# A banded attention, router and expert kernel: the exponential one group later, routing steps behind the maxima and in front of weights' low halves

## The chip, the cores and the metric

The kernel runs on one core of a Trainium2 chip. The metric is the device time of one execution in microseconds (us); lower is better. The engines are named as in the profile: PE is TensorE (matrix products; PEld its weight loads), DVE is VectorE, ACT is ScalarE, POOL is GpSimd, SP is the engine that only issues DMAs. Each engine takes its instructions in the order in which the program gave them.

## The reference, cut to what matters

Three stages in a row, with batch 4, sequence 576 and width 512:

```python
# 8 heads of 64; a band of 32 keys, heads 4 to 7 with a dilation of 4
scores = where(mask, q @ k.T / 8, -1e9)
attn = exp(scores - max) / (sum + 1e-9)
x = (attn @ v)                                  # (4, 576, 512)

# 8 experts of 512 x 1024 x 512, one per token
logits = x @ w_gate                             # gate from x @ w_local
e = argmax(logits[b, s]) if s == 0 or sigmoid(x @ w_local) < 0.5 else prev_e
x = p[e] * (relu(x @ w1[e]) @ w2[e])            # p = softmax(logits)

# a causal convolution of 5 taps as a gate
out = (sigmoid(conv(x)) * (x @ w_val)) @ w_out
```

The expert of a token can be that of the token before it, so the router holds a running maximum over the sequence; then the tokens of each expert are counted and gathered.

## The kernel before

**Attention.** The work is 8 iterations `it` (a pair of batches and a pair of heads each), each cut into five groups, so 40 groups (`NG`); a group has two slices of 128 queries, the fifth one. The loop at L1036 runs over `t`, the group whose scores are made, and in each turn works on several groups at different stages:

- `stage_a(t)` (L558): the score products into PSUM tile `s`, then on DVE one masked maximum per head and slice (L576, written `CUSTOM_DVE_ANT_0` with its `DVE_READ_ACCUMULATOR2_ANT` in the profile, `ISA` in the order), four in a group of two slices. They write `sm` and `mx`.
- `transpose_qk` for the next iteration: transposes of q and k on PE; k's are copied into `kbd` by ACT (L550, L553).
- `stage_sub(t)` (L580): POOL subtracts the maxima (L584). POOL also copies the q tiles of later iterations (`qside`, L489) and issues the gathers of tokens (L325).
- `stage_d` and `stage_l` (L641, L652): the finished attention rows are transposed, copied to `xT` by ACT (L650), and multiplied with the router's weights into `lp` (L661).
- `stage_b(t - 2)` (L594): transposes of the exponentials `pb` into `pt`, copied to `ph` by ACT or DVE (L603, L605).
- `stage_c(t - 3)` (L621): the product with v into `o`; after three slices `o_evac` (L609) normalises with three DVE instructions (`rc`, `rc`, `xsb`).
- `shift_v` (L511), a copy on ACT, in two groups of five; then `stage_exp(t)` (L587), the exponential on ACT, which needs POOL's subtraction of the same group.

So ACT's order in a turn is `kbd`, `xT`, `ph` of group t - 2, the shift, the exponential of group t, then high halves of weights.

**Routing among it.** `route(0)` (L762) is the router's work for the first two batches, begun at group `START` = 25. It gives small DVE instructions to a list (`Later`, L685). `later.tick(n)` takes the next n off the list and issues them: one after each maximum (L577), one after each step of the normalisation (L614, L616, L619), and `REST` = 3 at the end of a turn (L1147). In a profile they carry L716 or L701. Between them stand four products on PE (`lg`, `wp`, `bt`, `tb`); how many of the three calls of `later.passed()` in a turn must pass before a product's result is copied out of PSUM is `EVACUATE` = 2. The last of these products, `tb`, gives the table `tab`, from it the indices `idxa` by which tokens are gathered, and `eka2`, the number of the second expert.

**The first expert's weights.** Each expert has eight pieces of 128 x 1024 in f32, loaded into three slots `wst` (SP, L262, L265) and split in two f16 halves: ACT makes the high half `wh` (`split_a`, L274), DVE the low half `wl` (`split_b`, L279), which frees the slot, so that the load three pieces on is issued. `SPLIT` gives for each piece the groups at whose end the two are issued, the low halves (`finish_splits`) in front of the `REST` routing steps. The tokens come by POOL's gathers at groups 36, 37, 37 and 39, are transposed (`xt`, L337) and split (`xh`, `xl`); the first expert product `h` (L356) is issued at group 42.

After the attention come the experts, L356 and L405, and the last stage (L1427 to L1542). Nothing of their order is touched.

Of the kernel before, what the change touches and what calls it, by code (L numbers as in the profile page):

```python
# [53 lines left out]
BUSY = 40  # L54
RELIEF = 6
FILL = (6, 16)
SPLIT = ((34, 35), (34, 35), (35, 36), (37, 38), (38, 39), (39, 42), (41, 43), (41, 42), (45, 46), (47, 48), (48, 50), (51, 52), (52, 57), (55, 59), (57, 61), (61, 63))
GATHERS = (36, 37, 37, 39)
TURNS = (39, 40, 40, 43)
UP = (42, 43, 44, 44, 45, 46, 46, 47)  # L60
# [4 lines left out]
PREP = (18, 20, 22)  # L65
PLACES = (1, 2, 0, 0)
LAGS = (0, 3, 0, 2, 0, 0, 2)
EVACUATE = 2
START = 25
REST = 3  # L70
TICKS = (8, 6, 7, 4)
# [91 lines left out]
def attention_moe_conv_kernel(ctx: ExitStack, tc: tile.TileContext, q, k, v, w_gate, w_local, w1, w2, w_val, conv_w, w_out, consts, out):  # L163
# [112 lines left out]
    def split_b(k, i):  # L276
        wh, wl = wt[k, i]
        st = wf.pop((k, i))
        V.scalar_tensor_tensor(out=wl, in0=st, scalar=SW, in1=wh, op0=ALU.mult, op1=ALU.subtract)  # L279

    def start_splits(t):
        for n, (at, _) in enumerate(SPLIT):
            if t == at:
                split_a(2 * (n // 8), n % 8)

    def finish_splits(t):
        for n, (_, at) in enumerate(SPLIT):
            if t == at:
                split_b(2 * (n // 8), n % 8)
                k, i = 2 * ((n + 3) // 8), (n + 3) % 8  # L290
                if n + 3 < 16:
                    fetch_w(k, i, evs[k])
# [145 lines left out]
    if True:  # L438
# [15 lines left out]
        for n in range(2):  # L454
            flat = lv.tile([P, W + 4 * S], F32, name=f"kbd{n}")
            (V if n == 0 else G).memset(flat[:, 0:W], 0.0)
            t = flat[:, W:].rearrange("c (b h s) -> c b h s", b=2, h=2)
# [6 lines left out]
        def pair(it):  # L464
            return it // 4, PR[it // 4][it % 4]
# [89 lines left out]
        def scores(nm):  # L555
            return sp.tile([P, 2, 2, KB], F32, tag="s", name=nm)

        def stage_a(g):  # L558
            it, sl = groups[g]
            bp, pr = pair(it)  # L560
            dil = pr >= 2
            qT, (kb, front) = qk[it]
            qf = qT.rearrange("c b s -> c (b s)")
            ps = scores(f"s{g}")
            for n, s in enumerate(sl):
                for half in range(2):
                    blk = 2 * s + half
                    bl, i = divmod(blk, NB)
                    T.matmul(ps[64 * half : 64 * half + 64, n, :, :], lhsT=qf[:, QB * blk : QB * blk + QB], rhs=kb[:, bl, :, ks[i] : ks[i] + KB] if i else front[:, bl, :, 0:KB], start=True, stop=True)  # L569
            sm = wk.tile([P, 2, 2, KB], F32, tag="sm", name=f"sm{g}")  # L570
            mx = wk.tile([P, 4], F32, tag="mx", name=f"mx{g}")
            for n, s in enumerate(sl):
                mi = 3 + s if dil else (0 if s == 0 else 2 if s == 4 else 1)
                for h in range(2):
                    u = 2 * n + h
                    V.tensor_tensor_reduce(out=sm[:, n, h, :], in0=ps[:, n, h, :], in1=masks[:, KB * mi : KB * mi + KB], scale=0.125, scalar=-3e38, op0=ALU.add, op1=ALU.max, accum_out=mx[:, u : u + 1])  # L576
                    later.tick()  # L577
            stiles[g] = sm, mx

        def stage_sub(g):  # L580
# [6 lines left out]
        def stage_exp(g):  # L587
            ns = len(groups[g][1])
            smf = ptiles[g]
            pb = wk.tile([P, 4, KB], F32, tag="pb", name=f"pb{g}")  # L590
            A.activation(out=pb[:, 0 : 2 * ns, :], in_=smf, func=AF.Exp)
            ptiles[g] = pb
# [16 lines left out]
        def o_evac(it, part):  # L609
            bp, pr = pair(it)  # L610
            o = otile.pop((it, part))
            r = wk.tile([P, 3, 2], F32, tag="rc", name=f"rc{it}{part}")
            V.tensor_scalar(out=r, in0=o[:, :, :, HD], scalar1=1e-9, scalar2=None, op0=ALU.add)
            later.tick()  # L614
            V.reciprocal(out=r, in_=r)
            later.tick()  # L616
            xo = xsb[bp, pr >= 2][:, 3 * part : 3 * part + 3, P * (pr % 2) : P * (pr % 2) + P].rearrange("p s (h d) -> p s h d", h=2)
            V.tensor_tensor(out=xo, in0=o[:, :, :, 0:HD], in1=r.unsqueeze(3).to_broadcast([P, 3, 2, HD]), op=ALU.mult)
            later.tick()  # L619

        def stage_c(g):  # L621
            it, sl = groups[g]
# [62 lines left out]
        class Later:  # L685
# [55 lines left out]

            def passed(self):
                self.passes += 1
                if self.passes >= EVACUATE:
                    self.early()

            def slot(self):
# [11 lines left out]
        later = Later()  # L759
# [233 lines left out]
        NG = len(groups)  # L993
# [16 lines left out]
        with tc.manual_schedule():  # L1010
# [25 lines left out]
            for t in range(NG + 5):  # L1036
# [22 lines left out]
                    later.start(route(0))  # L1059
                later.passed()  # L1060
                later.product(0)
                if 0 <= t - 2 < NG:
                    stage_b(t - 2)

# [11 lines left out]
                if t < NG:  # L1076
                    if gi in ((1, 4) if it < 5 else (0, 3)):
                        shift_v(it, gi // 3)
                    stage_exp(t)
                start_splits(t)  # L1080

                if gi == 0 and 0 < it and it + 1 < 8:
# [54 lines left out]
                for j in (0, 2):  # L1137
                    if f"expert{j}" in later.marks and (j == 0 or t >= EXPERT2):
                        later.marks.remove(f"expert{j}")
                        evs[j] = nc.values_load(eka[j][0:1, 0:1], engines=[ET.SP], min_val=0, max_val=E - 1)  # L1140
                        for i in range(0 if j else 3):
                            fetch_w(0, i, evs[0])
                finish_splits(t)
                if "places" in later.marks:
                    later.marks.remove("places")
                    assert t <= GATHERS[0]
                later.tick(REST)  # L1147
                events(t)
                for at in UP:
                    if t == at and t < 44:  # L1150
# [482 lines left out]
```

## Time and profile before

| | before |
|---|---|
| median of 3 runs | 455.64 us (455.29 to 455.97) |
| the profiled execution | 456.03 us |
| its span, first to last instruction | 454.2 us |
| PE busy | 435.0 us, 96% of the span |
| DVE busy | 337.5 us, 74% |
| ACT busy | 291.9 us, 64% |
| POOL busy | 161.6 us, 36% |

All times inside the kernel are from the span's start. The attention and the first router take up to about 129 us, the experts up to about 340, the last stage the rest. Busy shares are means over these stages; what an engine waits for is read within a stage.

### The profile page before, as it was taken

The page shows a single profiled execution, that of the slowest core. Times are in us where ns is not written, and L with a number is a line of the kernel's source. Part 1 is how long each engine was busy: PE and PEld are TensorE (multiplying, and loading weights), DVE is VectorE, ACT ScalarE, POOL GpSimd, SP SyncE. Part 2 cuts the span into 40 slices and gives each one's busy share as a digit, 9 for nine tenths or more (in the row PEclk, how much of TensorE's full clock was granted, in tenths as well). Part 3 has the DMA queues.
Part 4 walks back from the last instruction along what each step waited for, and adds up shares of the span by engine and source line. Part 5 has one row for each costly group of instructions (what it writes and reads, how often), then busy time and mean ns, then how long its engine had stood idle before and what let it go on. Part 6 is the DMA issues. An engine that isn't in the chain of part 4 may idle for free. (4 is left out here: it accounts for less than half of the span.)

```text
span 454.2 us, 12091 instructions
## 1 busy us (share of the span) xinstructions
PE 435.0 (96%) x4618; PEld 324.1 (71%) x4618; DVE 337.5 (74%) x981; ACT 291.9 (64%) x590; POOL 161.6 (36%) x190
## 2 busy tenths in 40 slices
PE   8889999988699999999999999999999999999997
PEld 7567777766476688876788888788685757566664
DVE  5767787996788845788979999997038888779730
ACT  3877888766755434556566766766357998786532
POOL 3666655421600244102215133242115745434130
PEclk9999999996899999999999999999999999999999
DMA  9976698564847494366878898981052423020202
GB/s 207 202 178 150 156 244 200 143 182 137 253 116 277 174 319 150 114 239 221 218 271 286 280 316 240 312 262 36 9 175 84 150 70 105 25 93 5 91 23 94
DMA packets 56870, 77.32 MB, mean 170 GB/s; under 512 B 25810, under 2 KB 34146, under 8 KB 56808
## 3 DMA queue, kind: packets, MB, share of 16 engines
q1 hardware_dynamic: 53432, 66.72, 49.9%
q0 software_dynamic: 3232, 9.72, 6.2%
q8 instruction: 38, 0.62, 0.6%
q14 instruction: 24, 0.20, 0.1%
q10 hardware_dynamic: 144, 0.07, 0.1%
HBM read 62.19 MB, written 14.30 MB: 168 GB/s over the span
## 5 line engine op out<-in xcount | busy, mean ns | idle before, releaser
L356 PE MATMUL h<-xh,wh 128*128 128x256 f16 (+9 forms) x352 | 86.4, 256 | 1.4 <-DVE hl L360 1.2
L356 PE MATMUL h<-xl,wh 128*128 128x256 f16 (+9 forms) x352 | 86.4, 255 | 0.1
L356 PE MATMUL h<-xh,wl 128*128 128x256 f16 (+9 forms) x352 | 86.4, 256 | 0.0
L279 DVE SCALAR_TENSOR_TENSOR wl<-wst,wh 128x1024 f16<-128x1024 f32 x64 | 77.9, 1220 | 10.7 <-ACT wh L274 10.6
L1480 DVE SCALAR_TENSOR_TENSOR acc<-y,cw,acc 128x288 f32<-128x288 f32 x128 | 65.6, 520 | 9.2 <-ACT acc L1454 6.3
L356 PEld LDWEIGHTS <-wh 128*128 128x128 f16 x704 | 64.2, 98 | 9.4 <-issue 2.9
L274 ACT ACTIVATE wh<-wst 128x1024 f16<-128x1024 f32 x64 | 66.9, 1050 | 1.6 <-DMA wst<-in_moe_w_dram 1.6
L358 ACT ACTIVATE hh<-h 128x256 f16<-128x256 f32 (+9 forms) x88 | 30.6, 348 | 40.7 <-PE h L356 38.1
L360 DVE SCALAR_TENSOR_TENSOR hl<-h,hh 128x256 f16<-128x256 f32 (+9 forms) x88 | 32.4, 376 | 25.8 <-ACT hh L358 25.2
L584 POOL TENSOR_TENSOR sm<-sm,mx 128x384 f32<-128x384 f32 (+1 forms) x40 | 31.6, 792 | 51.6 <-DVE mx L576 32.5
L367 POOL DMA_INDIRECT yD<-yr,idx x15 | 18.1, 1208 | 82.6 <-ACT yr L366 54.9
L405 PE MATMUL yf<-wh,hh 128*128 128x512 f16 x104 | 39.4, 379 | 0.1
L405 PE MATMUL yf<-wh,hl 128*128 128x512 f16 x104 | 39.4, 379 | 0.0
L405 PE MATMUL yf<-wl,hh 128*128 128x512 f16 x104 | 39.4, 379 | 0.0
L1510 PE MATMUL v<-yh,wv_h 128*128 128x288 f16 x128 | 36.6, 286 | 0.3 <-DVE gg L1519 0.2
L1510 PE MATMUL v<-yh,wv_l 128*128 128x288 f16 x128 | 36.6, 286 | 0.0
L1510 PE MATMUL v<-yl,wv_h 128*128 128x288 f16 x128 | 36.6, 286 | 0.0
L356 PEld LDWEIGHTS <-wl 128*128 128x128 f16 x352 | 34.4, 98 | 2.5 <-issue 0.2
L405 PEld LDWEIGHTS <-hh 128*128 128x128 f16 x208 | 20.3, 98 | 21.1 <-issue 0.6
L576 DVE CUSTOM_DVE_ANT_0 sm<-s,masks 128x96 f32<-128x96 f32 x144 | 29.7, 251 | 6.8 <-PE s L569 5.5
L569 PE MATMUL s<-kbd,qT 128*64 128x192 f32 x288 | 31.8, 333 | 2.8 <-ACT kbd L553 2.0
L389 PEld LDWEIGHTS <-wh 128*128 128x128 f16 x576 | 32.9, 97 | 2.2
(248 smaller groups left out, 1052.7 us busy)
## 6 DMA issues: line engine op xcount, KB each, us to landing
wst<-in_moe_w_dram SPq DMA_DIRECT2D x64, 512.0 KB
qraw<-in_q_dram SPq DMA_DIRECT2D x16, 288.0 KB
kraw<-in_k_dram SPq DMA_DIRECT2D x16, 288.0 KB
out_dram<-ob SPq DMA_DIRECT2D x17, 256.0 KB
yg<-yD SPq DMA_DIRECT2D x16, 256.0 KB
xD<-xsb SPq DMA_DIRECT2D x2, 1152.0 KB
lraw<-in_moe_w_val_dram SPq DMA_DIRECT2D x4, 512.0 KB
lraw<-in_moe_w_out_dram SPq DMA_DIRECT2D x4, 512.0 KB
```

Of the source, the lines that this page charges most:

```text
L274: A.activation(out=wh, in_=st, func=AF.Copy, scale=SW)
L279: V.scalar_tensor_tensor(out=wl, in0=st, scalar=SW, in1=wh, op0=ALU.mult, op1=ALU.subtract)
L356: T.matmul(ps[:, :n], lhsT=w[:, fs], rhs=x[:, cc, :], start=q == 0, stop=q == 11)
L358: A.activation(out=hh[:, fc, :], in_=ps[:, :n], func=AF.Relu)
L360: V.scalar_tensor_tensor(out=hl[:, fc, :], in0=ps[:, :n], scalar=0.0, in1=hh[:, fc, :], op0=ALU.max, op1=ALU.subtract)
L389: T.matmul(ps[:, :r], lhsT=w[:, ds_], rhs=x[:, fc, r0:n], start=q == 0, stop=q == 23)
L405: T.matmul(ps, lhsT=x[:, fc, t0 : t0 + P], rhs=w[:, (fc % 2) * D : (fc % 2) * D + D], start=q == 0, stop=q == 23)
L569: T.matmul(ps[64 * half : 64 * half + 64, n, :, :], lhsT=qf[:, QB * blk : QB * blk + QB], rhs=kb[:, bl, :, ks[i] : ks[i] + KB] if i else f ...
L576: V.tensor_tensor_reduce(out=sm[:, n, h, :], in0=ps[:, n, h, :], in1=masks[:, KB * mi : KB * mi + KB], scale=0.125, scalar=-3e38, op0=ALU. ...
L584: G.tensor_tensor(out=smf, in0=smf, in1=mx[:, 0 : 2 * ns].unsqueeze(2).to_broadcast([P, 2 * ns, KB]), op=ALU.subtract)
L1480: V.scalar_tensor_tensor(out=acc, in0=y32[:, cc, s0 + k : s0 + k + hw], scalar=cw[:, cc, k : k + 1], in1=acc, op0=ALU.mult, op1=ALU.add)
L1510: T.matmul(ps, lhsT=w[:, cc, cs], rhs=x[:, cc, hs], start=q == 0, stop=q == 11)
```

## The change

1. `stage_exp(t)` at the end of a turn becomes `stage_exp(t - 1)` in the next turn, in front of `stage_b(t - 2)`.
2. The ticks after the single maxima are taken together after a group's last maximum, and those between the steps of the normalisation after its last step. The number of ticks is the same.
3. The `REST` routing steps stand in front of the low halves of the turn, not behind them.
4. In `SPLIT`, the low halves of pieces 1 and 2 of the first expert move from groups 35 and 36 to 36 and 37.
5. `EVACUATE` becomes a table by product: 2, 2, 2 and for the fourth 1.

```diff
-SPLIT = ((34, 35), (34, 35), (35, 36), (37, 38), (38, 39), (39, 42), ...
+SPLIT = ((34, 35), (34, 36), (35, 37), (37, 38), (38, 39), (39, 42), ...
-EVACUATE = 2
+EVACUATE = (2, 2, 2, 1)
...
                     V.tensor_tensor_reduce(out=sm[:, n, h, :], ...
-                    later.tick()
+            later.tick(2 * len(sl))
...
             V.tensor_scalar(out=r, in0=o[:, :, :, HD], scalar1=1e-9, scalar2=None, op0=ALU.add)
-            later.tick()
             V.reciprocal(out=r, in_=r)
-            later.tick()
...
             V.tensor_tensor(out=xo, in0=o[:, :, :, 0:HD], ...
-            later.tick()
+            later.tick(3)
...
-                if self.passes >= EVACUATE:
+                if self.passes >= EVACUATE[min(self.made, 4) - 1]:
...
                 later.product(0)
+                if 0 < t <= NG:
+                    stage_exp(t - 1)
                 if 0 <= t - 2 < NG:
                     stage_b(t - 2)
...
                         shift_v(it, gi // 3)
-                    stage_exp(t)
                 start_splits(t)
...
-                finish_splits(t)
+                later.tick(REST)
                 if "places" in later.marks:
                     later.marks.remove("places")
                     assert t <= GATHERS[0]
-                later.tick(REST)
+                finish_splits(t)
                 events(t)
```

ACT around group 34, before: the shift of v, then the exponential of group 33 (`pb33` from `sm33`), then what the turn of group 34 needs.

```order
L514 COPY vraw3False_1888<-vraw3False_1888 32x2x8x64
L591 ACTIVATE pb33_2073<-sm33_2033 128x384
L553 COPY kbd1_149<-tpk7_7_2087 64x288 x2
L650 COPY xT5_1931<-tpx52_2094 128x384
L603 COPY ph32_2104<-pt32_2099 96x512
L591 ACTIVATE pb34_2119<-sm34_2083 128x192
L274 ACTIVATE wh0_0_2121<-wst0_0_2017 128x1024
L274 ACTIVATE wh0_1_2124<-wst0_1_2019 128x1024
```

The same place in the changed kernel:

```order
L514 COPY vraw3False_1886<-vraw3False_1886 32x2x8x64
L553 COPY kbd1_149<-tpk7_7_2085 64x288 x2
L648 COPY xT5_1929<-tpx52_2092 128x384
L591 ACTIVATE pb33_2097<-sm33_2031 128x384
L603 COPY ph32_2104<-pt32_2099 96x512
L274 ACTIVATE wh0_0_2119<-wst0_0_2015 128x1024
L274 ACTIVATE wh0_1_2122<-wst0_1_2017 128x1024
L591 ACTIVATE pb34_2168<-sm34_2081 128x192
L603 COPY ph33_2175<-pt33_2170 96x512
```

The two copies into `kbd` and the copy into `xT` now stand ahead of the exponential of group 33, and two high halves ahead of that of group 34.

DVE at the end of group 35 and the start of group 36, before: the normalisation, the copy of the table, two low halves, then the place list and the first maximum.

```order
L613 TENSOR_SCALAR rc61_2185<-o6_1_2114 128x6
L615 RECIPROCAL rc61_2185<-rc61_2185 128x6
L618 TENSOR_TENSOR xsb6_2062<-o6_1_2114,rc61_2185 128x3x128
L716 COPY tab_78<-tb0_2153 128x48
L279 SCALAR_TENSOR_TENSOR wl0_0_2122<-wst0_0_2017,wh0_0_2121 128x1024
L279 SCALAR_TENSOR_TENSOR wl0_1_2125<-wst0_1_2019,wh0_1_2124 128x1024
L716 TENSOR_TENSOR pra_2190<-sel_112,tab_78 128x32
L701 TENSOR_REDUCE idxa_2191<-pra_2190 128x4
L576 ISA sm36_2225,mx36_2226<-s36_2220,masks_64 128x96
L576 ISA mx36_2226 128x1
L716 TENSOR_TENSOR pe02_2228<-sel_112,cst_63 128x8
```

The same place in the changed kernel:

```order
L714 COPY tab_78<-tb0_2151 128x48
L613 TENSOR_SCALAR rc61_2188<-o6_1_2114 128x6
L614 RECIPROCAL rc61_2188<-rc61_2188 128x6
L616 TENSOR_TENSOR xsb6_2062<-o6_1_2114,rc61_2188 128x3x128
L714 TENSOR_TENSOR pra_2178<-sel_112,tab_78 128x32
L699 TENSOR_REDUCE idxa_2179<-pra_2178 128x4
L714 TENSOR_TENSOR pe02_2212<-sel_112,cst_63 128x8
L699 TENSOR_REDUCE eka2_115<-pe02_2212 128x1
L279 SCALAR_TENSOR_TENSOR wl0_0_2120<-wst0_0_2015,wh0_0_2119 128x1024
L576 ISA sm36_2223,mx36_2224<-s36_2218,masks_64 128x96
```

The copy of `tab` stands in front of the normalisation, the place list and the expert's number in a row in front of the low half of piece 0, and piece 1's low half is no longer here.

SP at groups 35 and 36, before: the load of piece 4 of the first expert (`wst0_4`), four stores of attention rows, the read of the second expert's number, the load of piece 5.

```order
L265 DMA wst0_4_2216<-in_moe_w2_dram 128x2x512
L682 DMA xD_57<-xsb4_1466 32x256
L682 DMA xD_57<-xsb4_1466 112x256
L682 DMA xD_57<-xsb4_1466 16x256
L682 DMA xD_57<-xsb4_1466 128x256
L1140 TENSOR_LOAD eka2_115
L1140 ISA x2
L265 ISA
L265 DMA wst0_5_2273<-in_moe_w2_dram 128x2x512
```

The same place in the changed kernel:

```order
L680 DMA xD_57<-xsb4_1466 32x256
L680 DMA xD_57<-xsb4_1466 112x256
L680 DMA xD_57<-xsb4_1466 16x256
L680 DMA xD_57<-xsb4_1466 128x256
L1139 TENSOR_LOAD eka2_115
L1139 ISA x2
L265 ISA
L265 DMA wst0_4_2273<-in_moe_w2_dram 128x2x512
```

The load of piece 4 has moved behind the stores and the read.

## Rows read from the trace of the kernel before

**Rows 1.** Busy time by stretch (us): each engine, granted PE clock, DMA share, GB/s.

```profile
84.00:104.00 20.00, 16.52 (x228) 12.32 (x232) 18.73 (x110) 14.90 (x32) 7.07 (x11) 0.97 0.60 175
104.00:108.50 4.50, 4.50 (x54) 3.60 (x48) 0.70 (x6) 3.27 (x6) 0.83 (x1) 0.50 0.38 100
108.50:118.00 9.50, 7.08 (x84) 4.50 (x80) 9.16 (x44) 4.41 (x9) 4.21 (x4) 0.94 0.60 173
118.00:126.00 8.00, 5.97 (x57) 3.90 (x59) 4.78 (x11) 7.29 (x13) 3.79 (x5) 0.79 0.77 249
...
129.00:180.00 51.00, 50.55 (x579) 39.59 (x576) 36.05 (x101) 22.33 (x49) 11.69 (x10) 1.00 0.65 218
```

**Rows 2.** Timeline of PE: start, duration (us), line, operation, [idle before <-releaser].

```profile
103.67 1.19 PE L661 MATMUL lp<-xT,wg 128*32 128x144 f32 x16 [2.06 <-ACT xT L650]
...
119.20 0.55 PE L649 MATMUL tpx<-cst,xsb 128*128 128x128 f32 x3 [1.56 <-ACT xT L650]
...
121.56 1.12 PE L337 MATMUL xt<-cst,xg 128*128 128x128 f32 x4
...
125.29 0.55 PE L649 MATMUL tpx<-cst,xsb 128*128 128x128 f32 x3 [0.83 <-ACT ph L603]
...
126.38 1.10 PE L337 MATMUL xt<-cst,xg 128*128 128x128 f32 x8
...
129.11 0.28 PE L356 MATMUL h<-xh,wh 128*128 128x256 f16 x1
```

**Rows 3.** Timeline of ACT, groups 33 to 36.

```profile
101.73 0.52 ACT L591 ACTIVATE pb<-sm 128x384 f32<-128x384 f32 x1 [1.60 <-POOL sm L584]
...
103.13 0.48 ACT L650 COPY xT<-tpx 128x384 f32<-128x384 f32 x1
...
115.01 0.52 ACT L591 ACTIVATE pb<-sm 128x384 f32<-128x384 f32 x1 [3.76 <-POOL sm L584]
```

**Rows 4.** Timeline of DVE, its waits from group 35 on.

```profile
104.92 0.45 DVE L666 TENSOR_TENSOR lacc<-lacc,lp 128x288 f32<-128x288 f32 x1 [0.68 <-PE lp L661]
108.49 0.16 DVE L613 TENSOR_SCALAR rc<-o 128x6 f32<-128x6 f32 x1 [3.12 <-PE o L637]
...
118.81 1.23 DVE L279 SCALAR_TENSOR_TENSOR wl<-wst,wh 128x1024 f16<-128x1024 f32 x1 [0.91 <-ACT wh L274]
...
121.24 0.17 DVE L613 TENSOR_SCALAR rc<-o 128x6 f32<-128x6 f32 x1 [0.85 <-PE o L637]
```

**Rows 5.** Timeline of DVE: maxima alone, maxima with a step between, steps alone.

```profile
65.57 0.25 DVE L576 CUSTOM_DVE_ANT_0 sm<-s,masks 128x96 f32<-128x96 f32 x1
...
65.75 0.25 DVE L576 CUSTOM_DVE_ANT_0 sm<-s,masks 128x96 f32<-128x96 f32 x1
...
92.63 0.24 DVE L576 CUSTOM_DVE_ANT_0 sm<-s,masks 128x96 f32<-128x96 f32 x1
...
92.89 0.24 DVE L576 CUSTOM_DVE_ANT_0 sm<-s,masks 128x96 f32<-128x96 f32 x1
...
154.02 0.16 DVE L716 SCALAR_TENSOR_TENSOR key<-cnt,cst 128x8 f32<-128x8 f32 x1
154.22 0.17 DVE L716 SCALAR_TENSOR_TENSOR key<-big,key 128x8 f32<-128x8 f32 x1
```

**Rows 6.** Timeline of POOL and of DVE at the end of group 31.

```profile
93.78 0.83 POOL L584 TENSOR_TENSOR sm<-sm,mx 128x384 f32<-128x384 f32 x1 [2.23 <-DVE sel L716]
...
93.82 0.82 DVE L716 TENSOR_TENSOR pe<-sel,cst 128x8 f32<-128x8 f32 x1
```

**Rows 7.** Timeline of SP and of ACT: a weight load and the split that waited for it.

```profile
133.96 0.59 SPq L262 DMA_DIRECT2D wst<-in_moe_w_dram  x1
...
143.36 1.06 ACT L274 ACTIVATE wh<-wst 128x1024 f16<-128x1024 f32 x1 [1.36 <-DMA wst<-in_moe_w_dram]
```

**Rows 8.** Timeline of PE in the first groups.

```profile
13.08 0.86 PE L569 MATMUL s<-kbd,qT 128*64 128x192 f32 x6 [1.49 <-ACT kbd L553]
```

More of the change, by code (lines that the diff above doesn't have):

```diff
@@ L56 @@
 FILL = (6, 16)
-SPLIT = ((34, 35), (34, 35), (35, 36), (37, 38), (38, 39), (39, 42), (41, 43), (41, 42), (45, 46), (47, 48), (48, 50), (51, 52), (52, 57), (55, 59), (57, 61), (61, 63))
+SPLIT = ((34, 35), (34, 36), (35, 37), (37, 38), (38, 39), (39, 42), (41, 43), (41, 42), (45, 46), (47, 48), (48, 50), (51, 52), (52, 57), (55, 59), (57, 61), (61, 63))
 GATHERS = (36, 37, 37, 39)
```

## The prediction

> **What bounds the kernel now.** I read the busy time by stretch first. From 129 us to the end the TensorE is busy for all but a few per cent (50.55 of 51.00 us up to 180 [rows 1]) and runs its products back to back, so what starts there earlier ends earlier, and nothing there is touched by the change. From 84 to 126 us it is different: the TensorE has holes, its granted clock falls to 0.50 (1.2 instead of 2.4 GHz) in 104 to 108.5 us and to a mean of 0.79 in 118 to 126, and the VectorE is busy for 18.73 of 20 us up to 104 and for 9.16 of 9.5 us in 108.5 to 118 [rows 1]. So the VectorE bounds two pieces, and between them something else holds both engines.
>
> Second, the TensorE's waits [rows 2]. 2.06 us before the router's product lp at 103.67, released by the ScalarE's copy xT; 1.56 at 119.20, again by xT; 0.83 at 125.29, by the ScalarE's copy ph. Each time the ScalarE is late, and its rows say why [rows 3]: it sat 1.60 us in front of exp(33), which waits for GpSimd's subtraction, and the copy xT that the TensorE needed stood behind that in the queue and ran at 103.13. It sat 3.76 us in front of exp(36). After the first of these holes the clock is 0.50, so the TensorE's products up to 109 us take twice as long, and the VectorE waits for them: 0.68 us at 104.92 and 3.12 at 108.49 [rows 4]. Later it waits 0.91 us for a weight's high half (behind an exponential on ScalarE) and 0.85 for group 36's product o, which ran at half rate [rows 4].
>
> **The change part by part.** No instruction is added or removed; the order on TensorE and GpSimd is the same. What moves is ScalarE, VectorE, and one weight load on SP.
>
> *Exponential one group later.* exp(33) now stands behind kbd and xT of group 34, whose inputs the TensorE made before it stopped. Without the idle 1.60 us and the 0.52 of the exponential in front of them [rows 3] they end some 2.1 us earlier, xT at 101.5 instead of 103.6, and lp starts when the TensorE reaches it at 101.6: the 2.06 us go, and with them the hole that came before the half rate. The 4.5 us of TensorE work in 104 to 108.5 [rows 1] would take half of that at 2.4 GHz, 2.25 less. These two (up to 4.3) can't all be had, since the VectorE is next: it is busy without a pause until 102. Its two waits, 0.68 + 3.12 = 3.80 us [rows 4], are what it can give, and I take that as the gross gain of this stretch. In the first groups the same move frees kbd from exp(0): the TensorE waited 1.49 us there [rows 8]. I take 0, bounds 0 and 1.5: the next tiles of q reach the TensorE by a load and a copy on GpSimd, and neither is moved.
>
> *Routing steps behind the maxima and the normalisation.* Between two maxima a step cost little: maxima alone follow each other every 0.18 us, with a step between every 0.26 (92.63 to 92.89), so 0.08 a step. In a row, dependent steps follow each other every 0.20 us (154.02 to 154.22) [rows 5]. So a step that loses its place between others costs about 0.12 us more; bounds 0 (where another wait hides it) and 0.20 (where none of it was paid for before). From the order, 13 small steps lose it up to the tables (the four large one-hot steps cost the same either way), 5 after them. Three of the 13 fall before the VectorE's last idle moment ahead of the tables and cost nothing; 10 × 0.12 = 1.2 us lie on the bounding engine, and 5 × 0.12 = 0.6 later. In exchange the maxima of a group end some 0.25 us earlier, and so does the subtraction; that helps the chain, not the sum.
>
> *Low halves behind the routing steps, and two of them a group later.* wl(1) moves from group 35 to 36, wl(2) from 36 to 37. Each is 1.2 us of VectorE work in either place: 0 in the sum of the VectorE, but maxima of 36 come in front of two of them. The place list wanted by the gathers is ready before wl(0). wl(3) no longer waits 0.91, and group 36's o, at full rate and behind an earlier ph, no longer costs 0.85 [rows 4].
>
> *Evacuation of the fourth product one pass earlier.* The copy of tab enters the VectorE before the normalisation instead of behind it. Its product ends on the TensorE before the o that the normalisation wants; 0.
>
> *SP.* Loads 4 and 5 of the first expert are issued when wl(1) and wl(2) are done, so a group later, and load 4 stands behind four stores of xD and the read of the second expert's number. By my estimate (from the normalisation at 108.49 − 2.6 = 105.9, with that itself 0.9, ten steps of 0.20, four maxima of 0.18 and two low halves of 1.23 [rows 4, 5] behind one another) wl(1) ends and load 4 starts near 112, and load 5 near 115; both are wanted about 4 us later by the ScalarE. I take 0; what it costs if they are late is a rival below.
>
> *After the attention.* From 121.6 to 129.11, where the first expert product starts [rows 2], the TensorE loses 0.83 us of waiting and 0.57 by half rate (four transposes xt took 1.12 us, where eight take 1.10 at 126.38 [rows 2]). Of these 1.4 I take 0.9, since the VectorE's work on the gathered tokens stays where it is and may hold part of it; bounds 0 and 1.4.
>
> Sum: 3.8 − 1.2 + 0.91 + 0.85 − 0.6 + 0.9 = 4.7 us. The profiled execution took 456.03 us (span 454.2 and 1.8 around it), the median of the runs is 455.64, 0.4 less. 456.03 − 4.7 − 0.4 gives 450.9.
>
> **The rivals.**
>
> *A. The subtraction now meets all the steps (gain shrinks).* A routing step with two SBUF inputs that ran beside GpSimd's subtraction took 0.82 us instead of 0.16, which is what a step of eight elements takes elsewhere [rows 5, 6]. Before, three of four steps ran ahead of the subtraction and the fourth met it; now all four stand behind the maxima, where it runs, often with a copy of q behind it on GpSimd. If a second step is held in each of five groups, 5 × 0.66 = 3.3 us go, and the gain is 1.4: 454.2. Against it: the first held step lasts as long as the subtraction, and the second is past it.
> The Trainium skill says under SBUF — State Buffer, Who interferes with whom, that a Vector instruction with two SBUF inputs and a GpSimd instruction that reads SBUF exclude each other, and that the later one waits for the whole of the other. The row of 0.82 agrees; by that rule one step a group is held, as before, which is my sum, and two where GpSimd has two instructions in a row, which is this rival.
>
> *B. Late weights (slower).* ScalarE takes its work in order, and the high halves of pieces 4 and 5 stand behind ph in groups 38 and 39. A weight load that was issued at 133.96 was waited for until 143.36, 9.4 us [rows 7]. If loads 4 and 5 take that long, behind the stores, they land at 121.4 and 124.4, 5.4 us after they are wanted; the ScalarE, and behind it exp and ph, stands for that long, and the TensorE gets another hole with half rate behind it (as before, 1 to 2 us): 450.9 + 5.4 + 1.5 = 457.8. Under 4 us it costs nothing; it turns to a loss when landing takes over 8 us. Against it: the ScalarE didn't wait for a weight in this stretch before.
>
> *C. Nothing changes.* The moved exponential is then late for the transposes of the probabilities, one group away instead of two, and the holes only change their releaser from xT to pt: 455.6. Against it: exp(33) would end near 102 and its transposes are due after lp and the router's table product, near 104.
>
> *D. More.* The VectorE's extra cost is at its lower bound (0 instead of 1.8), and the whole 1.4 of the end is gained: 4.7 + 1.8 + 0.5 = 7.0, which gives 448.6; with the 1.5 us of the first groups 447.1. Say 448.
>
> **How the numbers follow.** Forecast (449.2 to 452.8) 0.50; D, below 449.2, 0.15; A and other partial losses of the gain, 452.8 to 454.7, 0.16; C, 0.08; B 0.11. About 0.2%, 0.9 us, is what a measurement of this kernel can tell from no change. Faster by more: 0.50 + 0.15 + 0.16 = 0.81; within 0.08; slower 0.11. The range reaches from D's 448.0 to 455.6, where C lies; that leaves out some 0.05 below and 0.14 above.
>
> **What would show it.** Right: lp follows the scores of group 35 with a wait under 0.5 us; no half rate between 103 and 109; the VectorE's two waits of 0.68 and 3.12 gone; expert products start near 124.5 instead of 129.11; the time from there to the end unchanged within 0.5. Routing rows at 0.2 us each in a row, one of them per group near 0.8. Rival A: two rows per group near 0.8. Rival B: ScalarE idle in front of wh, released by the weight's DMA, before 126. Rival C: TensorE waits at pt, released by pb. I am wrong in the main step if the VectorE's waits are gone and the experts start no earlier, or if a new hole opens after 109 with the clock at 0.50 again.

## The result and the profile after

The changed kernel takes 451.89 us (median of 6 runs, 451.54 to 453.20), the kernel before, beside it, 455.81 (455.29 to 456.21). The ratio is 0.9919 with an interval of 0.9905 to 0.9933: 3.9 us less, where 4.7 were forecast. The profiled execution took 452.03 us, its span is 450.2, 4.0 less than that of before.

Stretch by stretch (columns: the stretch in us, its length, busy time of PE, PEld, DVE, ACT and POOL with the number of instructions, granted clock, DMA share, GB/s), the answers to [rows 1] are:

```profile
84.00:104.00 20.00, 18.00 (x248) 13.59 (x249) 18.41 (x102) 15.95 (x32) 7.08 (x11) 1.00 0.62 175
104.00:108.50 4.50, 4.23 (x63) 3.15 (x61) 4.14 (x22) 4.40 (x7) 0.83 (x1) 1.00 0.35 89
108.50:118.00 9.50, 6.38 (x78) 4.24 (x78) 9.20 (x44) 6.15 (x11) 6.86 (x7) 1.00 0.79 249
118.00:126.00 8.00, 6.54 (x85) 4.77 (x86) 5.11 (x11) 6.61 (x12) 2.36 (x2) 1.00 0.55 190
```

In this profile no stretch runs at half rate, and in 104 to 108.5 us the VectorE is busy for 4.14 of 4.5 us, where it was busy for 0.70 before [rows 1]. From 84 to 118 us it is busy for 92% or more of each stretch; in 104 to 108.5 the ScalarE (4.40) and the TensorE (4.23) are so too, so there no single engine can be named as the bound.

The TensorE's timeline (start, duration, engine, line, operation, what it writes and reads, and in brackets the idle time ahead of it and what ended that) answers to [rows 2]:

```profile
101.90 0.73 PE L659 MATMUL lp<-xT,wg 128*32 128x144 f32 x16 [0.54 <-ACT xT L648]
...
117.97 1.23 PE L659 MATMUL lp<-xT,wg 128*32 128x144 f32 x16 [1.53 <-ACT xT L648]
...
121.24 0.55 PE L647 MATMUL tpx<-cst,xsb 128*128 128x128 f32 x3 [1.46 <-ACT ph L603]
...
125.05 0.28 PE L356 MATMUL h<-xh,wh 128*128 128x256 f16 x1
```

lp waits 0.54 us instead of 2.06 (the prediction's sign was under 0.5). The first expert product h starts at 125.05 instead of 129.11 [rows 2], 4.06 earlier, and from there to the end of the span it is 325.15 us, before 325.09: the whole gain lies ahead of h. But two waits further on are new or longer: 1.53 before the next lp, and 1.46 where 0.83 stood.

The ScalarE in the same kernel, for [rows 3]:

```profile
101.37 0.48 ACT L648 COPY xT<-tpx 128x384 f32<-128x384 f32 x1
101.88 0.53 ACT L591 ACTIVATE pb<-sm 128x384 f32<-128x384 f32 x1
...
112.23 1.06 ACT L274 ACTIVATE wh<-wst 128x1024 f16<-128x1024 f32 x1 [1.12 <-DMA wst<-in_moe_w_dram]
...
116.50 1.06 ACT L274 ACTIVATE wh<-wst 128x1024 f16<-128x1024 f32 x1 [0.88 <-DMA wst<-in_moe_w_dram]
117.46 0.46 ACT L648 COPY xT<-tpx 128x384 f32<-128x384 f32 x1
```

exp(33) follows xT without a wait. The high halves of pieces 3 and 4 wait for their loads, which they did not do before, and the copy xT at 117.46 for which lp waits stands right behind the second of them. What that costs is read in the part on the prediction.

The VectorE, for [rows 4] and [rows 5]:

```profile
93.49 0.17 DVE L714 SCALAR_TENSOR_TENSOR key0b<-cnt,key 128x8 f32<-128x8 f32 x1
93.57 0.16 DVE L714 SCALAR_TENSOR_TENSOR key0c<-cnt,key 128x8 f32<-128x8 f32 x1
93.65 0.15 DVE L714 TENSOR_REDUCE m<-key 128x1 f32<-128x8 f32 x1
93.84 0.74 DVE L714 TENSOR_SCALAR sel<-key,m 128x8 f32<-128x8 f32 x1
...
105.66 0.17 DVE L613 TENSOR_SCALAR rc<-o 128x6 f32<-128x6 f32 x1 [0.22 <-PE o L635]
...
117.58 1.50 DVE L279 SCALAR_TENSOR_TENSOR wl<-wst,wh 128x1024 f16<-128x1024 f32 x1
```

The waits of 0.68 and 3.12 us have become one of 0.22. In the row of four routing steps the second and the third each follow after 0.08 us; the last, which reads its predecessor's m, comes 0.19 after it, and is then held for 0.74 beside GpSimd's subtraction (93.72 to 94.55). The last row is the low half of piece 4.

### The profile page after: what moved, and what is told of

Its sections match the earlier page's. It is cut to its first block, busy times and chain, and to the rows that moved or that the text cites. A ratio compares the mean times of both kernels' runs of the same rounds, so it can differ in the third digit from the quotient of the medians.

```text
span 450.2 us, 12103 instructions
## 1 busy us (share of the span) xinstructions
PE 433.9 (96%) x4618; PEld 323.6 (72%) x4618; DVE 338.3 (75%) x981; ACT 291.7 (65%) x590; POOL 167.7 (37%) x190
## 5 line engine op out<-in xcount | busy, mean ns | idle before, releaser
L576 DVE CUSTOM_DVE_ANT_0 sm<-s,masks 128x96 f32<-128x96 f32 x144 | 28.6, 252 | 8.6 <-PE s L569 6.8
L389 PE MATMUL y<-hh,wh 128*128 128x96 f16 (+6 forms) x288 | 34.3, 198 | 0.0
```

Of the source, the lines that this page charges most:

```text
L389: T.matmul(ps[:, :r], lhsT=w[:, ds_], rhs=x[:, fc, r0:n], start=q == 0, stop=q == 23)
```

## Experiments

Twelve runs were made in three series of four, each beside the kernel before on the same chip; only ratios and distances inside a profile are compared across the series. One of the twelve is the changed kernel again (whole_change), and exp_alone ran twice. In these series the kernel before took 461.2 to 462.5 us, not 455.8. Part of that has a place: in ten of the twelve profiles (none is of the kernel before) it takes 329.9 to 333.4 us from h to the end, in the other two 325.5 and 326.8. low_halves_back is one of the ten; its rows, then those of the changed kernel:

```profile
130.00:160.00 30.00, 28.06 (x232) 20.82 (x225) 22.85 (x69) 11.23 (x19) 8.37 (x6) 1.00 0.67 226
160.00:200.00 40.00, 37.81 (x476) 29.79 (x475) 24.75 (x62) 17.85 (x42) 6.65 (x7) 1.00 0.51 175
```

```profile
130.00:160.00 30.00, 29.55 (x248) 22.74 (x246) 25.42 (x74) 13.42 (x24) 9.52 (x6) 1.00 0.68 223
160.00:200.00 40.00, 39.85 (x563) 31.30 (x561) 25.31 (x65) 18.70 (x44) 8.41 (x9) 1.00 0.60 199
```

The TensorE is idle there for 3.5 us more, early in the experts, where no kernel differs. So beside each ratio I read the trace up to h: from the score products of group 35 (s35), which stand ahead of the hole, to h, and to the normalisation of group 35 (rc) between them. The last column says where, between s35 and h, the granted clock was 0.50. Each row is one profile, so a difference of some tenths of a us between rows is not shown to repeat.

| kernel | ratio, interval | s35 to rc | s35 to h | half rate, us |
|---|---|---|---|---|
| before | | 7.76 | 28.38 | 103-110, 120-124 |
| the whole change, first profile | 0.9919, 0.9905-0.9933 | 5.12 | 24.51 | none |
| whole_change | 0.9939, 0.9914-0.9963 | 5.09 | 26.03 | 116-120, 123-127 |
| exp_alone | 0.9891, 0.9862-0.9919 | 4.50 | 23.78 | none |
| exp_alone_again | 0.9883, 0.9844-0.9922 | 4.47 | 23.76 | none |
| steps_alone | 1.0001, 0.9973-1.0028 | 7.27 | 28.33 | 104-111, 118-125 |
| low_halves_back | 0.9891, 0.9858-0.9923 | 5.96 | 25.33 | 104-108 |
| fill_hole | 1.0055, 1.0027-1.0084 | 9.98 | 31.03 | 104-108, 121-128 |
| hole_filled | 1.0014, 0.9985-1.0042 | 8.14 | 28.79 | 117-125 |
| one_exp_late | 0.9937, 0.9910-0.9965 | 4.29 | 25.00 | 115-119 |
| one_exp_early | 0.9944, 0.9925-0.9963 | 7.16 | 26.54 | 105-109 |
| steps_between | 0.9854, 0.9809-0.9900 | 4.49 | 24.41 | none |
| one_low_half | 0.9847, 0.9804-0.9890 | 4.50 | 23.30 | none |
| low_halves_both | 0.9888, 0.9836-0.9941 | 4.51 | 23.70 | none |

**Which part does it.** exp_alone is the kernel before with all exponentials one turn later and nothing else:

```
                 later.product(0)
+                if 0 < t <= NG:
+                    stage_exp(t - 1)
...
-                    stage_exp(t)
```

> The kernel before with one part of the change: the exponential of a group is issued one turn later; routing steps, low halves and evacuation stay as before. My theory (the gain is the exponential's: xT no longer stands behind exp(33), so the hole in front of lp and the half rate behind it go, and the rest of the change costs the VectorE some 1.8 us): lp waits under 0.7 us, granted clock 1.0 in 104 to 108.5 us, time 450 to 452, as fast as the whole change or up to 1.5 us faster. Rival (the gain is that of the routing steps and low halves, by which the subtraction comes earlier): 454 to 456, with exp(33) waiting and a hole left.

Ratio 0.9891, and 0.9883 when it ran again. Its VectorE, then its TensorE:

```profile
104.31 0.16 DVE L613 TENSOR_SCALAR rc<-o 128x6 f32<-128x6 f32 x1 [0.62 <-PE o L637]
```

```profile
123.59 0.28 PE L356 MATMUL h<-xh,wh 128*128 128x256 f16 x1
```

The exponential alone brings the gain, and h stands 1.46 us earlier than with the whole change (125.05); half of that, 0.73, is already there at s35, the other half follows by the table. The granted clock is 1.00 all the way and lp waits for nothing, as the theory had it. steps_alone is the other side, the whole change without the move of the exponential:

```
-                if 0 < t <= NG:
-                    stage_exp(t - 1)
...
+                    stage_exp(t)
```

> The whole change but for the exponential, which stays at the end of its own turn. My theory: xT stands behind exp(33) as before, so the hole in front of lp (1.5 to 2.1 us) and the half rate stay, and the steps in a row cost the VectorE about 1 us: 455 to 457.5. Rival (routing steps and low halves carry the gain): 452 to 454, lp waits under 1 us.

Ratio 1.0001. The hole and the wait behind it are there, the wait shorter (1.72), since the VectorE comes there later: the steps stand in a row, and it waits 0.46 us for the product of the copy tab, which now stands in front:

```profile
103.09 0.71 PE L659 MATMUL lp<-xT,wg 128*32 128x144 f32 x16 [2.05 <-ACT xT L648]
```

```profile
107.45 0.16 DVE L613 TENSOR_SCALAR rc<-o 128x6 f32<-128x6 f32 x1 [1.72 <-PE o L635]
```

So the other four parts give no gain that a measurement can tell, with the exponential or without it.

**One exponential.** one_exp_late moves only that of group 33 in the kernel before; one_exp_early puts only that one back in the whole change:

```
 one_exp_late
+                if t == 34:
+                    stage_exp(33)
...
-                    stage_exp(t)
+                    if t != 33:
+                        stage_exp(t)
 one_exp_early
-                if 0 < t <= NG:
+                if 0 < t <= NG and t != 34:
                     stage_exp(t - 1)
...
+                if t == 33:
+                    stage_exp(33)
```

> The kernel before, with one exponential moved: that of group 33 is issued in the turn of group 34, in front of the copies ph. All other exponentials stay at the end of their turn. Theory (one hole before lp, the half rate behind it, the VectorE's waits of 0.68 and 3.12 us): lp waits about 0.5 us, no wait above 1 us before the normalisation of group 35, h 3 to 4 us earlier than in the kernel before, ratio 0.991 to 0.993. Rival (the gain is spread over many groups, whose copies all come earlier): h at most 1.5 us earlier, ratio 0.9965 or above.

> The whole change, with one exponential moved back: that of group 33 is issued at the end of its own turn, as before. Theory of the one hole: the ScalarE waits 1.6 us for the subtraction again, lp waits about 2 us, the VectorE waits 3 us or more in 104 to 109, h 3 to 4 us later than in the whole change, ratio 0.998 to 1.002. Rival (gain spread over many groups): h within 1 us of the whole change, ratio 0.994 or below.

One exponential moved (first its VectorE's row, then its TensorE's):

```profile
104.68 0.16 DVE L613 TENSOR_SCALAR rc<-o 128x6 f32<-128x6 f32 x1 [0.41 <-PE o L637]
```

```profile
125.39 0.28 PE L356 MATMUL h<-xh,wh 128*128 128x256 f16 x1
```

The normalisation comes 3.81 us earlier than in the kernel before [rows 4], h 3.72 earlier [rows 2], ratio 0.9937. That these lie so near the 3.80 us of the sum is in part luck: 0.34 us of the 3.81 is there already at s35 (100.39 instead of 100.73), and 0.41 of the VectorE's wait is left. By the table it is 3.47 up to rc and 3.38 up to h, where all exponentials bring 4.60 (exp_alone). The ratio expected was 0.991 to 0.993; the interval holds that and more.

One exponential put back:

```profile
103.86 0.72 PE L659 MATMUL lp<-xT,wg 128*32 128x144 f32 x16 [1.99 <-ACT xT L648]
```

```profile
108.21 0.17 DVE L613 TENSOR_SCALAR rc<-o 128x6 f32<-128x6 f32 x1 [1.72 <-PE o L635]
```

The hole is back (1.99 us), but the wait behind it is 1.72, not 3 or more, h is at 127.59, between the two profiles of the whole change (125.05 and 127.06) and the kernel before, and the ratio, 0.9944, is that of whole_change. My expectation (0.998 to 1.002) missed, and the rival's row (h within 1 us of the whole change) holds only against the profile that had half rates. Two things of the rows make the price smaller here: the half rate behind the hole lasts for 4 us, not 7, and the VectorE arrives later on its own, since the steps stand in a row and the copy of tab waits 0.47 us. By the ratios of this series, putting this one back cost nothing that can be told.

What the other exponentials give can be read by setting this run beside steps_alone, which differs from it by them alone: 0.9944 against 1.0001, intervals apart, and 26.54 us from s35 to h against 28.33, nearly all of it behind rc (a half rate of steps_alone at 118 to 125 in it). So they bring a good part of the whole gain, behind the place where the two waits stood; in the sum they stand only among the later terms.

**The whole change again.**

> The whole change, beside its parts on one chip. Expected by the theory (the exponential that is issued a group later closes the hole of 2.06 us before lp, and with it the VectorE's two waits of 3.80 us go): ratio to before 0.990 to 0.994, the first expert product h some 4 us earlier than before and the time from there to the end as before. If the chip rather than the kernel set the ratio of 0.9919 that was measured first, the ratio here lies outside 0.989 to 0.995.

Ratio 0.9939, as expected. Up to rc its profile agrees with the first one to 0.03 us; behind that it has two stretches at half rate, and h comes at 127.06, 2.05 us earlier than in the kernel before and not some 4:

```profile
108.50:118.00 9.50, 7.21 (x78) 4.67 (x74) 9.22 (x45) 6.61 (x12) 6.41 (x6) 0.91 0.83 245
118.00:126.00 8.00, 6.22 (x66) 4.54 (x66) 4.90 (x9) 5.64 (x11) 2.83 (x3) 0.71 0.61 214
```

The same instructions, once with no half rate and once with two stretches of it, differ by 1.5 us between s35 and h. The same is seen in low_halves_back, the whole change with the `SPLIT` of before:

```
-SPLIT = ((34, 35), (34, 36), (35, 37),
+SPLIT = ((34, 35), (34, 35), (35, 36),
```

> The whole change but for the low halves of pieces 1 and 2, which are issued in groups 35 and 36 as before, so loads 4 and 5 start a group earlier. In the changed kernel the ScalarE waited 1.12 and 0.88 us for these loads in front of the high halves of pieces 3 to 5 and the TensorE then 1.53 us for xT and 1.46 for ph. Theory of the late loads: both waits under 0.2 us and the time 0.5 to 2 us under the changed kernel's, 450 to 451.4. Rival (the maxima of 36 then come 1.2 us later, behind two low halves, and the chain of group 36 loses what the loads gain): the same time within 0.5, 451.4 to 452.4, or slower.

Ratio 0.9891. Up to 104 us the TensorE does there what it does in the whole change, lp waits 0.51 us, and yet four transposes take 1.03 us (0.62 in the whole change, at 104.38), at a mean clock of 0.62 in 104 to 108.5:

```profile
101.76 0.73 PE L659 MATMUL lp<-xT,wg 128*32 128x144 f32 x16 [0.51 <-ACT xT L648]
...
104.24 1.03 PE L600 MATMUL pt<-cst,pb 128*96 128x128 f32 x4
```

The half rate makes s35 to rc 5.96 us where it is 5.12 and 5.09 without it, in the same instructions.

What this run was made for came out as its rival had it. No high half waits for its load any more, yet from rc to h it takes 19.37 us, and 19.39 in the first profile of the whole change. The low half of piece 1 stands ahead of the maxima of group 36 again, so the ScalarE waits longer for the subtraction of that group instead (2.67 us, 1.25 in the whole change), and comes to the high half of piece 4 at 117.38, no earlier:

```profile
111.99 0.52 ACT L591 ACTIVATE pb<-sm 128x384 f32<-128x384 f32 x1 [2.67 <-POOL sm L584]
...
117.38 1.06 ACT L274 ACTIVATE wh<-wst 128x1024 f16<-128x1024 f32 x1
```

The ratio, 0.9891, can't be told from that of the whole change: the intervals overlap.

**Filling the hole.** Two kernels were to run dummy products of ones in the idle time before lp, in the kernel before: fill_hole 40 of them into lp's own PSUM tile, hole_filled 30 into a tile of the ring of o.

```
 fill_hole
             ps = psum(RINGS[1], it, [P, 2, 2, PP], f"lp{it}")
+            if it == 5:
+                for _ in range(40):
+                    T.matmul(ps..., lhsT=ones16, rhs=ones16, start=True, stop=True)
 hole_filled
+            if it == 5:
+                busy(30)
             ps = psum(RINGS[1], it, [P, 2, 2, PP], f"lp{it}")
```

> The kernel before with 40 products of ones (128 x 128, f16) added on the TensorE in front of the real products of lp in group 35, into the same PSUM tile, which the real ones overwrite; they run in the hole and wait for nothing. Theory (the half rate in 104 to 108.5 comes from the hole and costs the VectorE's 3.12 us wait): granted clock near 1.0 there, the wait before the normalisation at 108.5 falls by 2 us or more, time 453 to 454.2. Rival (the half rate comes from elsewhere, or the wait is that of the late ph and exp): clock 0.5 as before or the wait within 0.7 of 3.12, time 455 to 456.5.

> The kernel before, with 30 products of ones in front of lp of iteration 5, in a PSUM buffer that is free there, so that they run while the TensorE would wait 2.06 us for xT (the dummy products of fill_hole waited for xT themselves). Theory (the half rate of 104 to 109 follows from that idle hole): lp still starts when xT is there, granted clock 1.00 in 103 to 109, the VectorE's wait of 3.12 us before the normalisation of group 35 falls to about 1, the first expert product some 2 us earlier, ratio 0.994 to 0.997. Rival (the half rate does not hang on the hole): half rate in the same place, the wait of 3 us stays, the first expert product where it was or up to 1 us later, ratio 0.999 to 1.003.

Neither did what it was made for; both PSUM tiles came free only at the end of the hole, behind the copy xT and behind the normalisation that ends with xsb. First fill_hole, then hole_filled:

```profile
104.70 3.64 PE L659 MATMUL lp<-ones 128*128 128x128 f16 x40 [2.06 <-ACT xT L650]
```

```profile
104.88 1.85 PE L1026 MATMUL busy<-ones 128*128 128x128 f16 x30 [1.99 <-DVE xsb L618]
106.66 0.71 PE L663 MATMUL lp<-xT,wg 128*32 128x144 f32 x16
...
108.86 0.62 PE L600 MATMUL pt<-cst,pb 128*96 128x128 f32 x4
```

So the test whether a filled hole keeps the clock was not made. What they do show is a price: 3.64 us more on the TensorE behind the hole put s35 to h up by 2.65 and the ratio to 1.0055. And hole_filled had the hole, and then full rate up to 117 us (the transposes take 0.62); the VectorE nevertheless waited 1.92 and 2.25 us there, with lp behind the 1.85 us of added products.

**Steps, and the loads behind the low halves.** steps_between is the whole change with the steps back between the maxima and in the normalisation; one_low_half, besides, has the low half of piece 2 back in group 36, and low_halves_both that of piece 1 in group 35 too.

```
 steps_between
+                    later.tick()
-            later.tick(2 * len(sl))
...
+            later.tick()
             V.reciprocal(out=r, in_=r)
+            later.tick()
...
-            later.tick(3)
+            later.tick()
 one_low_half
+SPLIT = ((34, 35), (34, 36), (35, 36),
 low_halves_both
+SPLIT = ((34, 35), (34, 35), (35, 36),
```

> The whole change, but the routing steps stand again one by one between the maxima and between the steps of the normalisation. Theory that steps in a row cost the VectorE more than between other instructions (0.20 against 0.08 us; the exponential alone was ahead of the whole change by 1.46 us at the first expert product): h 0.7 to 1.5 us earlier than in the whole change, the last maximum of group 34 some 0.7 us earlier, ratio 0.001 to 0.003 below that of the whole change. Rival (the steps cost nothing, since GpSimd's subtraction starts earlier where they stand behind the maxima; what set the exponential alone ahead is the low halves and with them the loads of pieces 4 and 5): h within 0.4 us of the whole change, high halves of pieces 3 and 4 still waiting about 1 us each for their loads, and the same ratio.

> steps_between with the low half of piece 2 back in group 36, so that only that of piece 1 is a group later. Theory of the late loads (the high halves that wait for weights, 1.36 and 1.31 us in steps_between, hold the copies xT behind them, and those the TensorE): the second of these waits falls under 0.5 us and the first expert product comes 0.4 to 1 us earlier than in steps_between (124.56). Rival (the low halves ahead of the maxima of group 36 are what costs): no earlier, or later by up to 0.7.

> steps_between with the low halves of pieces 1 and 2 both back in their groups of before. Theory of the late loads: no high half waits for its load, the first expert product 0.5 to 1 us earlier than in steps_between (124.56), as in the exponential alone (123.59), ratio as there. Rival (low halves ahead of the maxima): the subtraction of group 36 late, the exponential behind it waits 2 to 3 us, the first expert product at 124.5 or later.

> The kernel before with all exponentials one turn later and nothing else, beside the next two on one chip. Theory: it is ahead of the whole change by the price of the steps in a row, so ratio 0.986 to 0.991 and the first expert product near 123.6 us where no half rate falls in front of it. If its lead in the first series was luck with the half rate: ratio 0.992 to 0.994.

s35 to rc falls from 5.12 to 4.49 us when the steps go back, and it is 4.47 to 4.51 in all five profiles that have the exponentials late and the steps between (but for 4.29 with one exponential): the row of steps costs 0.6 us in that stretch, and the ratio goes from 0.9939 to 0.9854 beside it. That is more than was expected, and more than the rows explain: from s35 to h the two profiles of that series differ by 1.62 us, the half rate of whole_change in it, the medians by 2.83 (459.37 and 456.54); where the rest lies no profile shows. By the rows without any half rate it is 0.1 us at h (24.51 and 24.41), as the rival of steps_between had it, since the high halves still wait. In steps_between the high halves of pieces 3 and 4:

```profile
111.33 1.06 ACT L274 ACTIVATE wh<-wst 128x1024 f16<-128x1024 f32 x1 [1.36 <-DMA wst<-in_moe_w_dram]
116.02 1.06 ACT L274 ACTIVATE wh<-wst 128x1024 f16<-128x1024 f32 x1 [1.31 <-DMA wst<-in_moe_w_dram]
```

In one_low_half the second has no wait:

```profile
111.35 1.06 ACT L274 ACTIVATE wh<-wst 128x1024 f16<-128x1024 f32 x1 [1.46 <-DMA wst<-in_moe_w_dram]
...
115.02 1.06 ACT L274 ACTIVATE wh<-wst 128x1024 f16<-128x1024 f32 x1
```

From rc to h it takes 19.92 us in steps_between and 18.80 in one_low_half, neither with half rate: with the low half of piece 2 in group 37 it is 1.1 us longer, as the theory of the late loads had it. Moving piece 1's back as well, in low_halves_both, gives 19.19, 0.4 more than one_low_half: there only piece 3 waits for its load, 0.34 us, but the exponential of group 36 waits 2.16 for its subtraction, so theory and rival each held in part. The way by which piece 2's low half delays the load of piece 4 is not settled. Its own slot takes the load of piece 5, and the load of piece 4 is issued at 110.39 us in steps_between and at 110.12 in one_low_half, so nearly alike; it lands 5.6 us after its issue in the one and at most 4.9 after it in the other. GpSimd's second gather, which moves its rows by DMA too, starts at 112.06 in the one and at 112.99 in the other; whether that is the cause was not tried. one_low_half has the shortest s35 to h and, at 0.9847, an interval (0.9804 to 0.9890) that does not touch that of whole_change, nor of the first measurement (the whole change did not run in its series). steps_between, exp_alone and low_halves_both can't be told from it by the ratio.

## Why the prediction was right, step by step

**The hole and the VectorE's waits (3.8).** They measured 3.58 in the changed kernel (0.22 us of the 3.80 is left), and 3.39 with one exponential alone (0.41 is left). The main step stands. One reason in it does not stand as strictly as it was put: that the half rate follows from the hole. Behind a wait of 1.99 to 2.06 us in lp's place it came in four of the five profiles that have that wait (not in hole_filled), and without it in one of nine (low_halves_back, 0.51 us of waiting). There it cost 0.84 us from s35 to rc. Of the 2.64 by which the change shortened that stretch, 1.80 were gained even so: up to there the greater part of the gain does not hang on the clock.

The size of the gain at h in the first profile has luck in it: that profile has no half rate up to h. whole_change, the same program, has a wait of 1.49 us at 121.70 and half rate on both sides of it. That is one of the signs by which I said I would be wrong (a new hole after 109 with the clock at 0.50). Its ratio was forecast right even so.

The Trainium skill says in TensorE: Matmul & The Clock Gate, What's actually happening, that the clock is set by how busy the array has lately been, over a window that runs freely and is not reset when a kernel starts, so that the moment of a change varies from run to run. The two profiles of the whole change agree that it varies; in them whole stretches came and went (none at half rate up to h, against 116 to 120 and 123 to 127 us).

**Steps in a row (-1.2).** Too dear: 0.6 by the table. From the copy of qT to the first maximum of group 34 it took 12.63 us before and 13.19 after, 0.56 more. I charged every step 0.20 us; only a step that reads the result of the one ahead of it takes 0.19, the others 0.08, as between maxima [rows 5]. Rival A (a second step held in each group) did not come: the rows from 88 to 112 us show one held step beside a subtraction, of 0.74 us at 93.84, 0.69 at 96.04 and 0.68 at 109.43, and none with two.

The Trainium skill's rule in SBUF — State Buffer, Who interferes with whom, was weighed for this in the prediction. The trace agrees: each of these three steps ends within 0.03 us of a subtraction on GpSimd, and what was held moved with the order (the four one-hot steps at 100.30 take 2.06 us, the one behind them 0.54 where it took 1.18).

**The normalisation of group 35** was put at 105.9 and came at 105.66. Two errors partly cancel there: the waits gave 0.22 us less than forecast, the steps cost some 0.5 less.

**wl(3), o, the later steps (+0.91 + 0.85 - 0.6 = 1.16).** From that normalisation to the low half of piece 4 it was 13.77 us and is 11.92: 1.85 less. The waits are gone, the steps' 0.6 is not to be seen.

**The end of the attention (+0.9).** This is the term that was mis-sized. From the low half of piece 4 (wl) to h it took 6.85 us and takes 7.47, 0.6 more instead of 0.9 less. The row of before:

```profile
122.26 1.23 DVE L279 SCALAR_TENSOR_TENSOR wl<-wst,wh 128x1024 f16<-128x1024 f32 x1
```

I counted the TensorE's own losses there (0.83 of waiting, 0.57 by half rate) as what could be won. But the TensorE waits for the copy ph in both kernels, so the ScalarE sets the end. Its high half of piece 4 and that ph, before:

```profile
121.19 1.04 ACT L274 ACTIVATE wh<-wst 128x1024 f16<-128x1024 f32 x1
...
124.66 0.58 ACT L603 COPY ph<-pt 96x512 f32<-96x512 f32 x1
```

After, where the high half starts at 116.50:

```profile
118.03 0.52 ACT L591 ACTIVATE pb<-sm 128x384 f32<-128x384 f32 x1
...
120.61 0.57 ACT L603 COPY ph<-pt 96x512 f32<-96x512 f32 x1
```

From ph to h it is 4.45 us before and 4.44 after. From the high half to ph it is 3.47 before and 4.11 after, 0.64 more, and that is all of the 0.6. What is new between them is the exponential of group 38, which the change put there: 0.43 us until the next copy starts, and 0.2 by which it waits for GpSimd. There its subtraction, the first of the two in this row, starts only behind the gathers and takes 0.84 us, up to 117.99:

```profile
117.15 2.29 POOL L584 TENSOR_TENSOR sm<-sm,mx 128x384 f32<-128x384 f32 x2
```

The wait of rival B is there too, at a small size, but ahead of this stretch. SP's rows (issue, duration):

```profile
108.43 0.36 SPq L262 DMA_DIRECT2D wst<-in_moe_w_dram  x1
...
111.73 0.41 SPq L265 DMA_DIRECT2D wst<-in_moe_w_dram  x1
```

The second is the load of piece 4, issued as estimated ("near 112"). The ScalarE reaches its high half at 115.62 and waits until 116.50, so landing took 4.8 us. I wrote that up to 4 us it costs nothing, had no row for an unhindered landing, and took 0. Piece 3, whose load I did not look at, waits too: issued at 108.43, landed at 112.23. Before, the load of piece 4 was issued at 111.88, hardly later, but wanted only at 121.19; it was the ScalarE that came 5.6 us earlier. Behind the wait stand xT and lp's 1.53. That it made h later in this kernel is not shown: the exponential of group 38 could not have started before its subtraction ended, and low_halves_back, where no high half waits, is no faster from rc to h. In steps_between, where that exponential follows xT without waiting for GpSimd, the end of the wait in one_low_half went with 1.1 us.

3.58 - 0.71 (0.56 of the steps and 0.15 by which the VectorE was later ahead of them, the copy of qT at 89.56 instead of 89.41) + 1.85 - 0.62 is 4.1, the 4.06 of h. The forecast for h was 124.5 by its terms, against 125.05. The end of the attention missed its term by 1.5 us, and the others came out 1.0 larger than forecast, so the sum is nearer than its terms. Rivals C and D did not come: the hole before lp did not merely change its releaser, and up to s35 the TensorE gained 0.2 us (100.54 instead of 100.73), not 1.5.

## What to carry to other kernels

An in-order engine that waits for one late input holds everything behind it that is ready: put what others wait for (here the copies kbd and xT) in front of the instruction with the late input, one turn later if its reader allows that. Size such a gain by the waits on the engine that bounds next, not by the hole, and count what the moved instruction holds up in its new place (here 0.6 us at the end). Try the parts of a bundle apart: four of the five here brought nothing together, and without two of them (the steps in a row, one low half later) the kernel was faster than with all, by intervals of two series. For each load behind a changed stretch write down its issue, its landing and the moment at which it will be wanted after the change: a gain ahead of a load makes that load late without moving it. Whether the wait costs anything depends on what else the instruction behind it waits for.

## What was not expected of the hardware

The granted clock differs between executions of the same instructions: none of 84 to 126 us at half rate in one profile of the whole change, two stretches in another, 1.5 us later at h. A profile without half rate is therefore no proof that a kernel avoids it, and one profile is not enough to price a hole.

In ten of twelve profiles of the later series the way from h to the end, in code that is the same in all, is some 5 us longer than in the first series; in low_halves_back, whose rows stand above, 3.5 us of that are idle time of the TensorE between 130 and 200 us. In exp_alone and one_exp_late the ScalarE waits 4.8 us in that stretch, and its row names "remote" as releaser, no engine of this kernel. The cause stays open.
